# Staging the second weight matrix's words in its own storage, and finding clusters by halves of the tokens, in a routed attention with an ELU layer

## The chip, the cores and the metric

The kernel runs on one core of a Trainium2 chip. The metric is the device time of one execution in microseconds (us). The engines are TensorE (PE; its weight loads are listed as PEld), VectorE (DVE), ScalarE (ACT), GpSimd (POOL) and SyncE (SP), which here issues all DMA transfers, in the order of its queue.

## The reference

Two stages follow each other. The first is attention over 4 batches and 8 heads, with 768 tokens of 64 values. Each query and each key belongs to the one of 16 clusters whose centroid is most similar, and a query sees only the keys of its own cluster. The second is a layer with ELU.

```
q_assign = argmax(einsum('bhsd,hcd->bhsc', q_n, c_n))      # 16 clusters
k_assign = argmax(einsum('bhsd,hcd->bhsc', k_n, c_n))
mask = q_assign[:, :, :, None] == k_assign[:, :, None, :]
scores = where(mask, q @ k.T / 8, -1e9)
attn = softmax(scores) @ v                                  # (4, 8, 768, 64)
x = attn.transpose(0, 2, 1, 3).reshape(3072, 512)
h = x @ w_in                                                # (512, 2048)
g = where(h > 0, h, exp(min(h, 0)) - 1)
out = g @ w_out                                             # (2048, 512)
```

q, k, v and the centroids arrive as 32-bit floats. `w_in` and `w_out` arrive as 64-bit floats, and the kernel makes 32-bit floats of their words itself.

## The kernel before, in words

The attention is cut into 32 blocks: batch, half of the query tokens (`HS` = 384), and pair of heads (`blocks`). For block n, `scores(n)` makes, for each of 6 key tiles, the products q·k and on top of them a large negative number where the clusters differ (L350 and L359), and ACT takes the exponential (L367). `values(n)` multiplies with v (L394), sums the rows (L384), and DVE takes the reciprocal (L409). From block 4 on DVE adds up the key tiles first (`sums`, L371 and L373).

The clusters of a batch are worked out by `similar(b, j)` and `assign(b, j)`, j = 0 for q and 1 for k: 16 matmuls with 32 columns (L294), transposes out of PSUM (L302), the largest of 16 (L311), the comparison (L312), and a transpose back to the one-hot tile `hot` (L322). `masks(n)` makes the query side `qm` of a block from `hot` (L328).

The layer runs `LAG` = 4 blocks behind: during block n its group n - 4 runs. Groups come in turn as four `hidden` (8 matmuls with `w_in` into two PSUM banks, L422; ACT exponential L431; POOL clamp L432; DVE `gT`, L435, which reads the two banks and so frees them) and as six `outer` (4 matmuls with `w_out` each, L448). All of `similar`, `turn` (transposes of q and k), `scores`, the row sums and `hidden` draw on one pool of three PSUM tiles (`banks`).

The two weight matrices come as 32 pieces of 128 x 512 numbers: 0 to 15 are `w_in`, 16 to 31 are rows 0 to 15 of `w_out`. A piece's words, twice as large, are put into a place by a DMA (`ask`, L219). Generator `weight_steps` makes one step per piece: ACT goes on with piece n - 1 (L229, L230), DVE begins piece n (L234, L237) and ends piece n - 1 (L240, L243), POOL multiplies it (L246); then the place of piece n - 1 is free, and `ask` requests the next words. `ex`, the exponents, has two buffers, so L237 of step n follows L246 of step n - 1.

There are seven places: two tiles of their own (`words0`, `words1`), and five made of rows 6 to 15 of the `w_out` tile itself, two rows each; rows 0 to 5 first hold raw q and k. As soon as a piece of `w_out` is asked for (`asked >= into`, L213), the five are given up and the two are left.

Each engine's order is the order in which the code calls it. In blocks 0 to 3, `weigh` makes four steps a block; in blocks 4 to 7 two after each of the group's calls, five calls with `finish`, so steps 16 to 25 in block 4 and the rest in block 5. At a batch's last block `similar` and `assign` of the next batch are put between the `outer` calls. At the start of the program both run whole for q, then for k, then `masks(0)`.

Of the kernel before, what the change touches and what calls it, by code (L numbers as in the profile page):

```python
# [9 lines left out]
F32 = mybir.dt.float32  # L10
BF16 = mybir.dt.bfloat16
# [3 lines left out]
Alu = mybir.AluOpType  # L15
# [3 lines left out]
P = 128  # L19
# [41 lines left out]
def main_path(ctx, tc, c, q, k, v, centroids, moe_w_in, moe_w_out, out):  # L61
    nc = tc.nc
    B, H, S, D = q.shape
    NC = centroids.shape[1]
    DM, DF = moe_w_in.shape
    NT = S // P
    HT = NT // 2
    HS = S // 2
    NPR = H // 2
# [21 lines left out]
    def banks():  # L91
        return short.tile([P, 2, 512], F32, name="banks", tag="banks")
# [6 lines left out]
    used = 0  # L99

    def take(n):
        nonlocal used
        used += n
        return spare[:, used - n : used]
# [64 lines left out]
    cTz = const.tile([P, NPR, 2, 2, NC], F32, name="cTz")  # L169
    nc.vector.memset(cTz, 0.0)  # L170
    for pr in range(NPR):
# [1 line left out]
            cTz[:, pr, :, pr % 2],  # L173
            cps[:, 2 * pr * NC : 2 * (pr + 1) * NC].rearrange("p (e c) -> p e c", e=2),
        )
    count = const.tile([P, 2 * B], F32, name="count")
    r_sum = const.tile([P, HS], F32, name="r_sum")
    d_sum = const.tile([P, 2 * len(pairs)], F32, name="d_sum")
    nc.gpsimd.memset(r_sum, 0.0)
# [20 lines left out]
    words, exps = {}, {}  # L200
    places = []
    asked = 0

    def ask():

        nonlocal asked
        while asked < len(pieces):
            to, src = pieces[asked]
            if not wide:
                nc.sync.dma_start(to, src)  # L210
                asked += 1
                continue
            if asked >= into:  # L213
                places[:] = [x for x in places if x[1]]
            if not places:
                return
            place, own = places.pop(0)
            w = place.bitcast(U32)
            nc.sync.dma_start(w, src.bitcast(U32))  # L219
            words[asked] = (w.rearrange("p (n w) -> p n w", w=2), place, own)  # L220
            asked += 1

    def weight_steps():

        for n in range(len(pieces) + 1) if wide else ():
            if n > 0:
                to = pieces[n - 1][0]
                ex = exps[n - 1]
                nc.scalar.activation(to, to.bitcast(U32), Act.Identity, scale=2.0**-20, bias=one)  # L229
                nc.scalar.activation(ex, ex, Act.Relu, scale=8.0, bias=off)  # L230
            if n < len(pieces):
                high = words[n][0][:, :, 1]
                e = exps[n] = loads.tile([P, WC], U32, name="ex", tag="ex", bufs=2)
                nc.vector.tensor_scalar(  # L234
                    pieces[n][0].bitcast(U32), high, 0xFFFFF, None, op0=Alu.bitwise_and
                )
                nc.vector.tensor_scalar(e, high, 0x7FF00000, None, op0=Alu.bitwise_and)  # L237
            if n > 0:
                w, place, own = words.pop(n - 1)
                nc.vector.scalar_tensor_tensor(  # L240
                    ex, w[:, :, 1], 0x80000000, ex, op0=Alu.bitwise_and, op1=Alu.bitwise_or
                )
                nc.vector.scalar_tensor_tensor(  # L243
                    to, w[:, :, 0], 2.0**-52, to, op0=Alu.mult, op1=Alu.add
                )
                nc.gpsimd.tensor_tensor(to, to, ex.bitcast(F32), op=Alu.mult)  # L246
                places.append((place, own))
                ask()
            yield

    for n in range(2):
        places.append((loads.tile([P, 2 * WC], F32, name="words", tag=f"words{n}"), True))
    while used + 2 * WC <= FC * DM:
        places.append((take(2 * WC), False))
    ask()
    rest = weight_steps()

# [7 lines left out]
    T, sim, hot, qm = {}, {}, {}, {}  # L265
# [16 lines left out]
        to = T[i, j].rearrange("p (h s) -> p h s", h=2)  # L282
        nc.scalar.copy(to, ps[:, :, :HS])  # L283

    def similar(b, j):
        sim[b, j] = route.tile([P, S], F32, name="sim", tag="sim", bufs=1)
        ps = banks()
        for x in range(2):
            for half in range(2):
                for e in range(2):  # L290
                    for g in range(2):
                        pr = 2 * g + x
                        at = 64 * e + 32 * g
                        nc.tensor.matmul(  # L294
                            ps[at : at + 32, half, :HS],
                            lhsT=cTz[:, pr, e].rearrange("p x c -> p (x c)"),
                            rhs=T[b * NPR + pr, j][:, half * HS : (half + 1) * HS],
                            start=(x == 0),
                            stop=(x == 1),
                        )  # L300
        for half in range(2):
            nc.vector.transpose(  # L302
                sim[b, j][:, half * HS : (half + 1) * HS], ps[:, half, :HS]
            )

    def assign(b, j):
        n = S // NC
        s = sim.pop((b, j)).rearrange("p (n c) -> p n c", c=NC)
        top = route.tile([P, n], F32, name="top", tag="top", bufs=1)
        oh = route.tile([P, S], BF16, name="oh", tag="oh", bufs=1)  # L310
        nc.vector.tensor_reduce(top, s, axis=Axis.X, op=Alu.max)  # L311
        nc.vector.scalar_tensor_tensor(  # L312
            oh.rearrange("p (n c) -> p n c", c=NC),
            s,
            1.0,
            top.unsqueeze(2).to_broadcast([P, n, NC]),
            op0=Alu.mult,
            op1=Alu.is_equal,
            accum_out=count[:, 2 * b + j : 2 * b + j + 1],
        )  # L320
        hot[b, j] = route.tile([P, S], BF16, name="hot", tag=f"hot{j}", bufs=1 + j)
        nc.vector.transpose(hot[b, j], oh)  # L322

    def masks(n):
        b, half, pr = blocks[n]
        qm[n] = route.tile([P, HS], BF16, name="qm", tag="qm", bufs=2)
        s = big[:, pr : pr + 1]
        nc.vector.tensor_scalar(  # L328
            qm[n],
            hot[b, 0][:, half * HS : (half + 1) * HS],  # L330
            s,
            s,
            op0=Alu.mult,
            op1=Alu.subtract,
        )
# [139 lines left out]
    LAG = 4  # L475
# [13 lines left out]
    for j in range(2):  # L489
        for pr in range(NPR):  # L490
            turn(pr, j)
        similar(0, j)
        assign(0, j)
    masks(0)

    for n in range(len(blocks) + LAG):
        b, at = n // NB, n % NB
        ahead = b + 1 < B
        if ahead and at in turns:
            for j in range(2):  # L500
                turn((b + 1) * NPR + turns[at], j)
        if n <= len(blocks) and n > 0:
            values(n - 1)
        if ahead:
            for pr in {0: [0], 1: [1], 2: [2], 5: [3]}.get(at, []):
                load("q", (b + 1) * NPR + pr)
                load("k", (b + 1) * NPR + pr)
        if n + 1 < len(blocks):
            load_v(n + 1)
        if n < LAG:  # L510
            weigh(1)
        if n < len(blocks):
            scores(n)
            if at + 1 < NB:
                masks(n + 1)
            if n >= LAG:
                sums(n)
        beside = []
        if ahead and at + 1 == NB:
            for j in range(2):  # L520
                beside.append(lambda b=b, j=j: (similar(b + 1, j), assign(b + 1, j)))
            beside.append(lambda n=n: masks(n + 1))
        main = groups[n - LAG] if n >= LAG else []
        if n < LAG:
            weigh(3)
        done = 0
        for m, step in enumerate(main):
            step()
            upto = len(beside) * (m + 1) // len(main)
            for other in beside[done:upto]:  # L530
                other()
            done = upto
            if n < LAG + 4:
                weigh(2)
        for other in beside[done:]:
            other()
# [2 lines left out]

    ok = c["ok"]  # L540
    peak = const.tile([P, 2], F32, name="peak")
    same = const.tile([P, 2 * B], F32, name="same")
    nc.vector.tensor_reduce(peak[:, 0:1], r_sum, axis=Axis.X, op=Alu.add)
    nc.vector.tensor_reduce(peak[:, 1:2], d_sum, axis=Axis.X, op=Alu.add)
    nc.vector.tensor_scalar(ok[:, 0:1], peak[:, 0:1], R_MAX, None, op0=Alu.is_lt)
    nc.vector.tensor_scalar(ok[:, 1:2], peak[:, 1:2], D_MAX, None, op0=Alu.is_lt)
    nc.vector.tensor_scalar(same, count, float(S // NC), None, op0=Alu.is_equal)
    nc.vector.tensor_reduce(ok[:, 2:3], same, axis=Axis.X, op=Alu.min)
    nc.vector.tensor_reduce(ok[:, 3:4], ok[:, 0:3], axis=Axis.X, op=Alu.min)
    ps = banks()[:, 0]  # L550
# [227 lines left out]
```

## Time and profile before

| | us |
|---|---|
| median of 3 runs (1116.4 to 1118.55) | 1118.15 |
| profiled execution | 1116.62 |
| its span, first to last instruction | 1114.8 |
| PE busy | 1053.9 (95%) |
| DVE busy | 423.0 (38%) |
| ACT busy | 319.1 (29%) |
| POOL busy | 202.0 (18%) |

Shares of busy time are means over the span. What an edit is worth is read from the stage that it touches: from the waits there, and from who is waited for. A matmul in 32 bits stands in the trace as two records. Matmul ends are modelled, and neighbouring rows of PE overlap a little. Times in rows count from the span's start.

### The profile page before, as it was taken

To read this page: it belongs to the slowest core of one execution; us is meant where nothing else is said; L and a number is where in the kernel's file an instruction comes from. 1 tells how busy PE (TensorE), PEld (TensorE's weight loads), DVE (VectorE), ACT (ScalarE), POOL (GpSimd) and SP (SyncE) were. 2 spreads that over 40 slices of the span, in tenths; PEclk is the share of its full clock that TensorE was granted. 3 is DMA by queue.
4 is the path that set the end of the run, shared out by engine and by line. 5 is a ranking of instruction groups with operands and counts; after the bars stand their busy time and mean duration, and the time that the engine had idled before them with its cause. 6 is when DMAs were issued, how large, how long until landed. Compare 5 with 4: busy or idle time off the path is not lost.

```text
span 1114.8 us, 10753 instructions
## 1 busy us (share of the span) xinstructions
PE 1053.9 (95%) x4443; PEld 529.5 (47%) x4443; DVE 423.0 (38%) x472; ACT 319.1 (29%) x475; POOL 202.0 (18%) x169
## 2 busy tenths in 40 slices
PE   6999384999999999999999999999999999999997
PEld 4445142444554455444554455544554455444543
DVE  4686464344431244344332344334343334330210
ACT  3774252222331132222321223321222223221100
POOL 0344233111220022111211122110221112110100
PEclk9999686999999999999999999999999999999999
DMA  9642342003010001003010001000000000000000
GB/s 274 177 123 75 97 118 69 15 24 90 15 43 24 34 15 28 15 24 91 14 43 10 24 24 43 15 24 34 11 4 14 34 24 15 15 10 19 1 0 32
DMA packets 61961, 49.05 MB, mean 44 GB/s; under 512 B 45520, under 2 KB 54736, under 8 KB 61904
## 3 DMA queue, kind: packets, MB, share of 16 engines
q1 hardware_dynamic: 61904, 48.28, 15.0%
q8 instruction: 37, 0.61, 0.2%
q14 instruction: 20, 0.16, 0.0%
HBM read 41.98 MB, written 6.29 MB: 43 GB/s over the span
## 4 chain that ended last, share of the span: by engine, by line
PE 84%; DVE 9%; DMA 5%; POOL 1%; ACT 1%; issue 0%; DVEq 0%; ACTq 0%
PE banks L422 26%; PE o_bank L448 20%; PE f_bank L448 10%; PE o_bank L394 10%; PE banks L350 10%; DMA words<-in_moe_w_out_dram 4%; PE banks L359 2%; PE banks L294 2%; DVE ex L240 2%; PE banks L384 2%; PE banks L275 1%; DVE r L409 1%; DVE ex L237 1%; POOL w_in L246 1%; DVE psum L373 1%; DVE w_in L243 1%
## 5 line engine op out<-in xcount | busy, mean ns | idle before, releaser
L422 PE MATMUL banks<-xT,w_in 128*128 128x384 f32 x1024 | 334.8, 488 | 2.4 <-POOL xT L410 2.3
L422 PEld LDWEIGHTS banks<-xT,w_in 128*128 128x128 f32 x1024 | 193.1, 190 | 142.1 <-issue 7.3
L448 PE MATMUL o_bank<-w_out,gT 128*128 128x512 f32 x512 | 227.3, 596 | 0.7 <-ACT o_sb L457 0.7
L409 DVE RECIPROCAL r<-r 128x384 f32<-128x384 f32 x32 | 81.7, 2552 | 311.5 <-ACT r L408 311.5
L350 PE MATMUL banks<-qT,kT 64*128 64x384 f32 x768 | 163.8, 505 | 6.2 <-ACT qT L283 3.8
L367 ACT ACTIVATE p<-banks 128x768 f32<-128x768 f32 x192 | 152.1, 812 | 23.1 <-PE banks L359 21.1
L448 PEld LDWEIGHTS o_bank<-w_out,gT 128*128 128x128 f32 x512 | 95.8, 190 | 123.7 <-issue 121.9
L373 DVE TENSOR_TENSOR psum<-psum,p 128x768 f32<-128x768 f32 x112 | 141.4, 1263 | 11.7
L410 POOL TENSOR_TENSOR xT<-xT,r 128x384 f32<-128x384 f32 x32 | 54.7, 1710 | 499.5 <-DVE r L409 499.5
L435 DVE SCALAR_TENSOR_TENSOR gT<-gT,banks 128x768 f32<-128x768 f32 x64 | 61.0, 954 | 216.0 <-POOL gT L432 216.0
L394 PE MATMUL o_bank<-p,v_raw 128*64 128x384 f32 x768 | 137.3, 499 | 2.7 <-ACT o_sb L457 2.7
L431 ACT ACTIVATE gT<-banks 128x768 f32<-128x768 f32 x64 | 51.9, 810 | 261.7 <-PE banks L422 261.7
L448 PE MATMUL f_bank<-w_out,gT 128*128 128x512 f32 x256 | 114.1, 593 | 0.0
L350 PEld LDWEIGHTS banks<-qT,kT 64*128 64x128 f32 x768 | 68.7, 192 | 63.8 <-issue 34.8
L432 POOL TENSOR_SCALAR gT<-gT 128x768 f32<-128x768 f32 x64 | 53.4, 835 | 249.2 <-ACT gT L431 249.2
L394 PEld LDWEIGHTS o_bank<-p,v_raw 128*64 128x64 f32 x768 | 53.2, 140 | 78.2 <-issue 72.0
L457 ACT COPY o_sb<-o_bank 128x512 f32<-128x512 f32 x16 | 9.4, 587 | 274.4 <-PE o_bank L448 274.4
L448 PEld LDWEIGHTS f_bank<-w_out,gT 128*128 128x128 f32 x256 | 48.4, 190 | 61.7 <-issue 61.7
L359 PE MATMUL banks<-qm,hot 64*128 64x384 bf16 x384 | 64.8, 330 | 3.6 <-DVE qm L328 3.6
L411 POOL TENSOR_TENSOR r_sum<-r_sum,r 128x384 f32<-128x384 f32 x32 | 52.4, 1637 | 0.0
L406 ACT COPY xT<-o_bank 128x384 f32<-128x384 f32 x32 | 15.3, 480 | 94.1 <-PE o_bank L394 94.0
L359 PEld LDWEIGHTS <-hot 64*128 64x128 bf16 x384 | 19.9, 96 | 29.8 <-DVE hot L322 3.9
(85 smaller groups left out, 448.7 us busy)
## 6 DMA issues: line engine op xcount, KB each, us to landing
v_raw<-in_v_dram SPq DMA_DIRECT2D x32, 384.0 KB, 3.1
words<-in_moe_w_out_dram SPq DMA_DIRECT2D x16, 512.0 KB, 3.5
out_dram<-o_sb SPq DMA_DIRECT2D x24, 256.0 KB, 2.0
k_raw<-in_k_dram SPq DMA_DIRECT2D x28, 192.0 KB, 4.7
w_out<-in_moe_w_in_dram SPq DMA_DIRECT2D x10, 512.0 KB, 6.3
q_raw<-in_q_dram SPq DMA_DIRECT2D x24, 192.0 KB, 4.4
words<-in_moe_w_in_dram SPq DMA_DIRECT2D x6, 512.0 KB, 4.6
q_raw<-in_q_dram SPq DMA_DIRECT2D x2, 384.0 KB, 3.5
```

Source lines behind the costliest of these rows:

```text
L350: nc.tensor.matmul(s[:, e, :HS], lhsT=T[i, 1][rows, ts(kt, P)], rhs=T[i, 0][rows, cols], start=True, stop=False,)
L359: nc.tensor.matmul(s[:, e, :HS], lhsT=hot[b, 1][rows, ts(kt, P)], rhs=qm[n][rows], start=False, stop=True,)
L367: nc.scalar.activation(p, s[:, :, :HS], Act.Exp, scale=SCALE)
L373: nc.vector.tensor_tensor(to, to, pu[n, kt], op=Alu.add)
L394: nc.tensor.matmul(o_bank[64 * e : 64 * e + 64, :HS], lhsT=raw["v", n][:, e, kt], rhs=pu[n, kt][:, e], start=(kt == 0), stop=(kt == NT - 1),)
L409: nc.vector.reciprocal(r, r)
L410: nc.gpsimd.tensor_tensor(x, x, r, op=Alu.mult)
L411: nc.gpsimd.tensor_tensor(r_sum, r_sum, r, op=Alu.add)
L422: nc.tensor.matmul(h[:, e, :HS], lhsT=w_in[:, ch, ts(2 * n + e, P)], rhs=xT[b * NPR + ch, half], start=(ch == 0), stop=(ch == KC - 1),)
L432: nc.gpsimd.tensor_scalar(t, t, 1.0, 0.0, op0=Alu.min, op1=Alu.max)
L435: lambda: nc.vector.scalar_tensor_tensor(t, t, -1.0, h[:, :, :HS], op0=Alu.add, op1=Alu.max)
L448: nc.tensor.matmul(o, lhsT=g[f // 2][:, f % 2, ts(t, P)], rhs=w_out[:, f], start=(f == 0), stop=(f == FC - 1),)
```

## The change

Four edits. First, a place carries a limit instead of a mark: a place in rows f and f + 1 of `w_out` may take words of any piece below 16 + f - 1, that is, of pieces which are finished before row f itself is begun. Second, the steps are handed out two after each of the first four calls of a group, in every block until none is left: steps 16 to 23 in block 4, 24 to 31 in block 5, 32 in block 6. Third, `similar` and `assign` work on half of the tokens, 384, and `masks(0)` stands between q and k. Fourth, at a batch's last block the calls of `similar` and `assign` are eight, spread singly between the `outer` calls.

```diff
-            if asked >= into:
-                places[:] = [x for x in places if x[1]]
+            places[:] = [x for x in places if asked < x[1]]
             if not places:
                 return
-            place, own = places.pop(0)
+            place, limit = places.pop(0)
...
     while used + 2 * WC <= FC * DM:
-        places.append((take(2 * WC), False))
+        limit = into + used // DM - 1
+        places.append((take(2 * WC), limit))
...
-    def similar(b, j):
-        sim[b, j] = route.tile([P, S], F32, name="sim", tag="sim", bufs=1)
-        ps = banks()
+    def similar(b, j, half):
+        if half == 0:
+            sim[b, j] = route.tile([P, S], F32, name="sim", tag="sim", bufs=1)
+        ps = banks()[:, 0]
+        cols = slice(half * HS, (half + 1) * HS)
...
-    def assign(b, j):
-        n = S // NC
+    def assign(b, j, half):
+        if half == 0:
+            hot[b, j] = route.tile([P, S], BF16, name="hot", tag=f"hot{j}", bufs=1 + j)
+        cols = slice(half * HS, (half + 1) * HS)
+        n = HS // NC
...
-        similar(0, j)
-        assign(0, j)
-    masks(0)
+        for half in range(2):
+            similar(0, j, half)
+            assign(0, j, half)
+        if j == 0:
+            masks(0)
...
-                beside.append(lambda b=b, j=j: (similar(b + 1, j), assign(b + 1, j)))
+                for half in range(2):
+                    beside.append(lambda b=b, j=j, half=half: similar(b + 1, j, half))
+                    beside.append(lambda b=b, j=j, half=half: assign(b + 1, j, half))
...
-            if n < LAG + 4:
+            if m < 4:
                 weigh(2)
```

SP's queue in blocks 2 to 4, as a difference (- before, + now); the two loads of v are those for blocks 4 and 5. `words` and `w_out` ahead of the arrow are the places that take the words of the last pieces.

```order
+L218 DMA w_out<-in_moe_w_out_dram 128x1024 x2
 L115 DMA v_raw<-in_v_dram 128x2x384
-L219 DMA words<-in_moe_w_out_dram 128x1024
+L218 DMA w_out<-in_moe_w_out_dram 128x1024 x3
+L218 DMA words<-in_moe_w_out_dram 128x1024
 L115 DMA v_raw<-in_v_dram 128x2x384
-L219 DMA words<-in_moe_w_out_dram 128x1024 x10
+L218 DMA words<-in_moe_w_out_dram 128x1024
+L218 DMA w_out<-in_moe_w_out_dram 128x1024 x3
+L218 DMA words<-in_moe_w_out_dram 128x1024 x2
```

The words of six `w_out` pieces (five of them into `w_out`) are are requested ahead of the second load of v, where before it was one.

DVE at the start of the program, from k's similarity on, before (`sim`, `hot` and `oh` numbered as buffers):

```order
L302 STREAM_TRANSPOSE sim_292<-banks_293 128x384 x2
L311 TENSOR_REDUCE top_312<-sim_292 128x48
L312 SCALAR_TENSOR_TENSOR oh_313,count_153<-sim_292,top_312 128x768
L322 STREAM_TRANSPOSE hot_316<-oh_313 128x768
L328 TENSOR_SCALAR qm_318<-hot_254,big_125 128x384
L234 TENSOR_SCALAR w_in_60<-words_161 128x512
```

and now, from the mask on:

```order
L329 TENSOR_SCALAR qm_262<-hot_241,big_125 128x384
L302 STREAM_TRANSPOSE sim_300<-banks_301 128x384
L312 TENSOR_REDUCE top_312<-sim_300 128x24
L314 SCALAR_TENSOR_TENSOR oh_313,count_153<-sim_300,top_312 128x384
L323 STREAM_TRANSPOSE hot_311<-oh_313 128x384
L302 STREAM_TRANSPOSE sim_300<-banks_317 128x384
L312 TENSOR_REDUCE top_327<-sim_300 128x24
L314 SCALAR_TENSOR_TENSOR oh_328,count_153<-sim_300,top_327 128x384
L323 STREAM_TRANSPOSE hot_311<-oh_328 128x384
L233 TENSOR_SCALAR w_in_60<-words_161 128x512
```

The mask `qm` now stands ahead of k's clusters, and k's first half is in `hot` after four instructions of half the size.

PE in the last block of a batch, before:

```order
L448 MATMUL o_bank<-w_out,gT 128x512 x8
L294 MATMUL banks<-qT,cTz 32x384 x16
L448 MATMUL o_bank<-w_out,gT 128x512 x8
L294 MATMUL banks<-kT,cTz 32x384 x16
L448 MATMUL f_bank<-w_out,gT 128x512 x8
```

and now:

```order
L449 MATMUL o_bank<-w_out,gT 128x512 x4
L295 MATMUL banks<-qT,cTz 32x384 x8
L449 MATMUL o_bank<-w_out,gT 128x512 x4
L295 MATMUL banks<-qT,cTz 32x384 x8
L449 MATMUL o_bank<-w_out,gT 128x512 x8
L295 MATMUL banks<-kT,cTz 32x384 x8
L449 MATMUL f_bank<-w_out,gT 128x512 x4
L295 MATMUL banks<-kT,cTz 32x384 x8
L449 MATMUL f_bank<-w_out,gT 128x512 x4
```

The two similarity stretches have become four of half the length, so `outer` is cut twice more.

## Rows read from the trace of the kernel before

**Rows 1.** Windows: stretch and length, busy us (instructions) by engine, PE clock, DMA.
```profile
core 0: us, PE busy (x) PEld busy (x) DVE busy (x) ACT busy (x) POOL busy (x), PEclk, DMA share, GB/s
...
88.00:144.00 56.00, 33.39 (x120) 17.73 (x118) 29.78 (x47) 20.22 (x31) 18.83 (x16) 0.80 0.31 92
144.00:196.00 52.00, 37.20 (x142) 20.18 (x140) 28.65 (x41) 19.97 (x31) 17.46 (x15) 0.79 0.32 93
```
**Rows 2.** Groups by form: busy us, mean ns | idle us before, and its releaser.
```profile
L234 DVE TENSOR_SCALAR w_out<-words 128x512 uint32<-128x512 uint32 x16 | 8.1, 508 | 44.3 <-DMA words<-in_moe_w_out_dram 44.3
```
**Rows 3.** Timeline of DVE, block 4: start us, us, engine, line [idle before <-releaser].
```profile
96.38 1.06 DVE L234 TENSOR_SCALAR w_out<-words 128x512 uint32<-128x512 uint32 x1
...
98.29 0.71 DVE L243 SCALAR_TENSOR_TENSOR w_in<-words,w_in 128x512 f32<-128x512 uint32 x1
102.47 0.43 DVE L234 TENSOR_SCALAR w_out<-words 128x512 uint32<-128x512 uint32 x1 [3.47 <-DMA words<-in_moe_w_out_dram]
...
103.75 0.69 DVE L243 SCALAR_TENSOR_TENSOR w_out<-words,w_out 128x512 f32<-128x512 uint32 x1
104.35 0.95 DVE L435 SCALAR_TENSOR_TENSOR gT<-gT,banks 128x768 f32<-128x768 f32 x1
```
**Rows 4.** Timeline of PE, blocks 4 and 5.
```profile
89.58 21.30 PE L422 MATMUL banks<-xT,w_in 128*128 128x384 f32 x64
116.25 1.54 PE L275 MATMUL banks<-ident,q_raw 128*128 128x128 f32 x6 [5.37 <-DVE gT L435]
127.06 1.54 PE L275 MATMUL banks<-ident,k_raw 128*128 128x128 f32 x6 [9.27 <-DVE gT L435]
...
138.10 1.49 PE L384 MATMUL banks<-psum,ones 128*64 128x384 f32 x4 [4.09 <-DVE gT L435]
...
195.11 0.81 PE L384 MATMUL banks<-psum,ones 128*64 128x384 f32 x4
...
200.90 3.70 PE L448 MATMUL o_bank<-w_out,gT 128*128 128x512 f32 x8
```
**Rows 5.** Timeline of DVE, block 1: two weight steps' first instructions.
```profile
50.27 0.43 DVE L234 TENSOR_SCALAR w_in<-w_out 128x512 uint32<-128x512 uint32 x1
...
53.42 0.42 DVE L234 TENSOR_SCALAR w_in<-words 128x512 uint32<-128x512 uint32 x1
```
**Rows 6.** Timeline of POOL, block 4.
```profile
96.33 0.83 POOL L432 TENSOR_SCALAR gT<-gT 128x768 f32<-128x768 f32 x1 [2.81 <-ACT gT L431]
...
104.57 1.27 POOL L246 TENSOR_TENSOR w_out<-w_out,ex 128x512 f32<-128x512 f32 x1 [4.23 <-issue]
```
**Rows 7.** Timeline of all engines at the program's start, from k's similarity on.
```profile
17.87 3.18 PE L294 MATMUL banks<-kT,cTz 128*32 128x384 f32 x32
...
21.11 1.05 DVE L302 STREAM_TRANSPOSE sim<-banks 128x384 f32<-128x384 f32 x2 [1.82 <-PE banks L294]
...
25.08 0.34 DVE L328 TENSOR_SCALAR qm<-hot,big 128x384 bf16<-128x384 bf16 x1
...
25.47 0.46 PE L359 MATMUL banks<-qm,hot 64*128 64x384 bf16 x2 [3.58 <-DVE qm L328]
...
29.16 3.23 ACT L367 ACTIVATE p<-banks 128x768 f32<-128x768 f32 x4 [0.78 <-PE banks L359]
...
33.64 0.69 DVE L240 SCALAR_TENSOR_TENSOR ex<-words,ex 128x512 uint32<-128x512 uint32 x1 [6.59 <-ACT ex L230]
```
**Rows 8.** Chain that ended last: start us, us, engine, tile, line, records.
```profile
242.57 7.06 PE o_bank L448 x16
...
376.72 6.87 PE f_bank L448 x16
```
**Rows 9.** DMA issues: tiles, KB each, median us to landing.
```profile
words<-in_moe_w_out_dram SPq DMA_DIRECT2D x16, 512.0 KB, 3.5
```
**Rows 10.** Timeline of PE, block 3: key tiles ahead of and behind an idle stretch.
```profile
69.52 0.81 PE L350 MATMUL banks<-qT,kT 64*128 64x384 f32 x4
...
72.38 0.92 PE L350 MATMUL banks<-qT,kT 64*128 64x384 f32 x4 [1.89 <-ACT p L367]
...
73.29 1.43 PE L350 MATMUL banks<-qT,kT 64*128 64x384 f32 x4
```

More of the change, by code (lines that the diff above doesn't have):

```diff
@@ L175, in main_path @@
         )
-    count = const.tile([P, 2 * B], F32, name="count")
+    count = const.tile([P, 4 * B], F32, name="count")
     r_sum = const.tile([P, HS], F32, name="r_sum")
@@ L212, in ask @@
                 continue
-            if asked >= into:
-                places[:] = [x for x in places if x[1]]
+            places[:] = [x for x in places if asked < x[1]]
             if not places:
                 return
-            place, own = places.pop(0)
+            place, limit = places.pop(0)
             w = place.bitcast(U32)
             nc.sync.dma_start(w, src.bitcast(U32))
-            words[asked] = (w.rearrange("p (n w) -> p n w", w=2), place, own)
+            words[asked] = (w.rearrange("p (n w) -> p n w", w=2), place, limit)
             asked += 1
@@ L238, in weight_steps @@
             if n > 0:
-                w, place, own = words.pop(n - 1)
+                w, place, limit = words.pop(n - 1)
                 nc.vector.scalar_tensor_tensor(
@@ L246, in weight_steps @@
                 nc.gpsimd.tensor_tensor(to, to, ex.bitcast(F32), op=Alu.mult)
-                places.append((place, own))
+                places.append((place, limit))
                 ask()
@@ L251, in main_path @@
     for n in range(2):
-        places.append((loads.tile([P, 2 * WC], F32, name="words", tag=f"words{n}"), True))
+        places.append((loads.tile([P, 2 * WC], F32, name="words", tag=f"words{n}"), len(pieces)))
     while used + 2 * WC <= FC * DM:
-        places.append((take(2 * WC), False))
+        limit = into + used // DM - 1
+        places.append((take(2 * WC), limit))
     ask()
@@ L283, in turn @@
         nc.scalar.copy(to, ps[:, :, :HS])
-    def similar(b, j):
-        sim[b, j] = route.tile([P, S], F32, name="sim", tag="sim", bufs=1)
-        ps = banks()
-        for x in range(2):
[L289 to L304, printed above, removed]
@@ L306, in assign @@
-    def assign(b, j):
-        n = S // NC
-        s = sim.pop((b, j)).rearrange("p (n c) -> p n c", c=NC)
+    def similar(b, j, half):
[3 more added lines that the diff above has]
+        cols = slice(half * HS, (half + 1) * HS)
+        for x in range(2):
+            for e in range(2):
+                for g in range(2):
+                    pr = 2 * g + x
+                    at = 64 * e + 32 * g
+                    nc.tensor.matmul(
+                        ps[at : at + 32, :HS],
+                        lhsT=cTz[:, pr, e].rearrange("p x c -> p (x c)"),
+                        rhs=T[b * NPR + pr, j][:, cols],
+                        start=(x == 0),
+                        stop=(x == 1),
+                    )
+        nc.vector.transpose(sim[b, j][:, cols], ps[:, :HS])
@@ L309, in assign @@
+    def assign(b, j, half):
[3 more added lines that the diff above has]
+        n = HS // NC
+        s = sim[b, j][:, cols].rearrange("p (n c) -> p n c", c=NC)
         top = route.tile([P, n], F32, name="top", tag="top", bufs=1)
-        oh = route.tile([P, S], BF16, name="oh", tag="oh", bufs=1)
+        oh = route.tile([P, HS], BF16, name="oh", tag="oh", bufs=1)
         nc.vector.tensor_reduce(top, s, axis=Axis.X, op=Alu.max)
+        at = 4 * b + 2 * j + half
@@ L318, in assign @@
             op1=Alu.is_equal,
-            accum_out=count[:, 2 * b + j : 2 * b + j + 1],
+            accum_out=count[:, at : at + 1],
         )
-        hot[b, j] = route.tile([P, S], BF16, name="hot", tag=f"hot{j}", bufs=1 + j)
-        nc.vector.transpose(hot[b, j], oh)
+        nc.vector.transpose(hot[b, j][:, cols], oh)
     def masks(n):
@@ L541, in main_path @@
     peak = const.tile([P, 2], F32, name="peak")
-    same = const.tile([P, 2 * B], F32, name="same")
+    same = const.tile([P, 4 * B], F32, name="same")
     nc.vector.tensor_reduce(peak[:, 0:1], r_sum, axis=Axis.X, op=Alu.add)
@@ L546, in main_path @@
     nc.vector.tensor_scalar(ok[:, 1:2], peak[:, 1:2], D_MAX, None, op0=Alu.is_lt)
-    nc.vector.tensor_scalar(same, count, float(S // NC), None, op0=Alu.is_equal)
+    nc.vector.tensor_scalar(same, count, float(HS // NC), None, op0=Alu.is_equal)
     nc.vector.tensor_reduce(ok[:, 2:3], same, axis=Axis.X, op=Alu.min)
```

## The prediction

> **What bounds the kernel now.** I read the windows first. Between 88 and 196 us TensorE (PE) is busy for 33.39 of 56 and 37.20 of 52 us, at mean granted clocks of 0.80 and 0.79 [rows 1]; after that it hardly stops. So 37.4 us of PE idle lie in blocks 4 and 5, where `w_out` is converted. Next, who waits there: VectorE (DVE) sat 44.3 us in front of the first instruction of a weight step, 14 times, for a transfer of words [rows 2]. The DVE timeline shows one such step: DVE stood still from 99.0 (98.29 + 0.71) to 102.47 and was done with the step at 104.35 [rows 3]. The PE timeline shows who pays: the turns of block 5 wait 5.37 and 9.27 us, and the row sums of block 4 wait 4.09 us, for PSUM banks that the ELU's last instruction, `gT` on DVE (L435), must free [rows 4]. `gT` stands behind two weight steps each time, so transfer → DVE → bank → PE is the chain. The last PE instruction that waits for it is the row sum of block 5, at 195.11; from 200.90 PE runs through [rows 4]. I use that row sum as the marker.
>
> A second chain is at the start: PE waits 3.58 us for the first mask, because DVE works out the clusters of all 768 k tokens before PE may use any [rows 7].
>
> **The change, part 1: words staged in `w_out`.** Before, from piece 16 on two places take turns, each asked for at the end of the step that frees it; a transfer lands in 3.5 us (median) [rows 9], nearly all of it waited for. Counting the requests of the new rule with its limits: pieces 16 to 22 are asked for seven places ahead, 23 to 27 with three or more steps between, 28 to 30 with one step and a `gT` between, piece 31 at the end of step 30, with nothing between. So all waits go but one.
>
> What is late next? A step without a wait for words takes 3.15 us (50.27 to 53.42) [rows 5]. Its four DVE instructions need 1.88 us (102.47 to 104.35) [rows 3], the rest is the multiply on GpSimd (POOL, L246, 1.27 us) [rows 6]: 1.88 + 1.27 = 3.15, so DVE and POOL take turns. In blocks 4 and 5 one `gT` and its clamp on POOL (L432) come to each pair of steps. `gT` and L246 overlapped at 104.35 and 104.57 with neither longer [rows 3, 6], so I cost `gT` at nothing, under L246; without that cover it would be 0.95 us a pair. The clamp is dearer: beside the one at 96.33 (0.83 us) the masking instruction L234 took 1.06 instead of 0.43 us [rows 3, 6]. So the pair costs between 2 × 3.15 = 6.3 us (clamp free) and 7.13 us (clamp in turn); I take 7.1, by that row. The Trainium skill (SBUF — State Buffer, Who interferes with whom) gives DVE and GpSimd one shared pair of ports, which whoever comes first holds for the whole instruction; by that rule 7.1 holds, and without a lock the sum below would be 5 us lower. The row of 1.06 us agrees. PE needs 5.3 us for a pair's matmuls (21.30 / 4) [rows 4], so the DVE–POOL chain remains the limit, not PE.
>
> Times on the old axis. Block 4: step 16 ends at 99.0 as before; step 17 ends at 102.15; its `gT` 0.95 later at 103.1; three more pairs to 124.4; row sum at 124.5 (138.10 before). Block 5: a row sum and the scores after it take 5.8 us (195.11 to 200.90) [rows 4], the first hidden pair 5.3: 135.6. In block 4 step 16 ended 4.1 us after its first hidden pair (89.58 + 5.3 = 94.9, to 99.0): step 24 ends at 139.7, step 25 at 142.85, the first `gT` at 143.8. Three pairs: 165.2. Piece 31's transfer adds 3.5 in place of the 1.27 of L246 that it hides: 167.4. Row sum at 167.5 instead of 195.11: **27.6 us gained**.
>
> Clock: PE still idles behind `gT`, some 2 us before the marker. At 72.38 an idle of 1.89 us was followed by key tiles at half clock, 1.43 instead of 0.81 us (1.2 GHz, the lower of its two levels) [rows 10]. I charge 2 us, between 0 and 3.5.
>
> The step that slips from blocks 4 and 5 into block 6 (eight steps a block instead of ten) finds DVE idle: costed at nothing, with `outer` of block 6 (20 us of PE) as cover. Requests pass the q, k and v loads on SP's queue, which wait for PE to free their buffers; those buffers are free a block earlier, so nothing is charged (rival B prices it).
>
> **Part 2: clusters by halves, at the start.** The sixteen matmuls of k's similarity run from 17.87 for 3.18 us; the first eight end near 19.5. DVE's chain for 768 tokens runs from 21.11 to the mask at 25.08, 4.0 us, so about 2.1 a half with its extra starts: first half at 21.7, second at 23.8. q's halves are done under k's turns, and the q mask now stands ahead of k. PE's scores reach the one-hot at 21.9 instead of 25.47 [rows 7]: 3.55 us. PE then no longer falls to half clock (three key tiles near 1.5 instead of 0.81 us), and the last exponential ends near 27.2 instead of 32.39 (29.16 + 3.23) [rows 7]. The first waiting weight instruction, at 33.64, moves to 28.5. **5.1 us gained**, between 2 (only DVE's end counts) and 5.5; from there to block 4 the chain is DVE and POOL without other slack, so it shifts whole. The words of the first pieces must then land some 2 to 5 us earlier than they were used; no row shows DVE waiting for them, and the low end of 2 us covers a wait.
>
> **Part 3: the same at the three batch ends.** PE runs through there, so the DVE time is covered by `outer` and by the next block's values, without which the last half's chain of 2.1 us would be paid. But the four similarity blocks now cut `outer` in four places instead of two. A stretch of 16 right after a cut took 7.06, one that goes on 6.87 [rows 8]: 0.19 a cut, 6 more cuts, **1.1 us lost**; up to 3.6 if entering the narrow matmuls costs twice as much again. The Trainium skill (TensorEngine Tiling, Key Properties) says that a change of tiling mode drains TensorE, which speaks against these cuts; counted for entry and exit at 0.19 each, an estimate, it would be 2.3 us. The rows show the exit; the entry no row separates.
>
> **Sum.** The profiled execution took 1116.62 us (span 1114.8), 1.5 below the median of 1118.15. 1116.6 − 27.6 + 2 − 5.1 + 1.1 = **1087.0 us**. A difference under 0.2% (2 us) can't be told from none here.
>
> **Rivals.**
> A: the waits go and DVE and POOL keep up, so PE sets the time in blocks 4 and 5. Then the 37.4 us idle goes and some 9 us of half clock with it (of at most 0.2 × 108 = 22): 46 us; 1116.6 − 46 − 5.1 + 1.1 = 1066.6. Needs a pair under 5.3 us. The step of 3.15 us speaks against it. 0.04.
> B: words come late again, because requests stand on SP behind loads that wait for PE, and pieces 23 to 30 each wait as 31 does, 3.5 − 1.27 = 2.2 us: 8 × 2.2 = 17.6 more, 1104.6. For it: DVE now asks in quick succession. Against: before, with the same loads in between, a request landed in 3.5 us all the same [rows 9]. 0.06.
> C: no place in `w_out` is really used beyond piece 16. Then only parts 2 and 3 act: 1116.6 − 5.1 + 1.1 = 1112.6; with the start gaining nothing either, no change. The order of SP's queue speaks against it. 0.02 (0.02 more for no change).
> D, slower: at the three batch ends the last half of k's clusters is late, since four similarity blocks now draw on three PSUM banks and the fourth must wait for DVE. Place: between `outer` and the next block's scores. PE has 3.4 us of `outer` and the values behind the last cut as slack; slower only if each of the three ends stalls by more than 10 us, 29.6 / 3. At 12 us each: 1087 + 36 = 1123. DVE's 2.1 us a half speak against it. 0.02.
> That the start gains only 2 us, or the clamp is free, is within the forecast.
>
> **How the numbers follow.** Forecast case 0.84: 1087. Low end: clamp free (6 × 0.83 = 5.0), start 5.5, no half clock (2), last transfer hidden (2.2): 1077.4. High end: start 2 (3.1 less), clock 3.5 (1.5), cuts 3.6 (2.5), clamp as long as L246 (6 × (1.27 − 0.83) = 2.6): 1096.7. The range 1077 to 1098 leaves out A, B, C and D, 0.16. Faster 0.95 (forecast, A, B, C and a little of the tails), same 0.02, slower 0.03.
>
> **What would show it.** In the profile after: no wait of DVE for words but one near the end of block 5, of some 3.5 us; weight steps at 3.1 us, pairs near 7.1; the block 5 row sum near 162; PE's mask wait at the start under 1 us; a cut of `outer` at 0.2 us. Wrong would be: several waits for words, a wait for sim or hot at a batch end, or PE without idle in blocks 4 and 5.

## The result, and the profile after

The changed kernel takes **1084.36 us** (median of 4 runs, 1083.68 to 1084.65), the kernel before 1118.35 us in the same comparison: a ratio of 0.9699, 95% interval 0.9682 to 0.9716. The forecast was 1087.0 us (1077 to 1098) and faster. The profiled execution took 1084.65 us with a span of 1082.9 us, 31.9 less than the 1114.8 before. Of these 31.9, the stages below show 2.7 at the start, 31.4 in blocks 4 and 5, and a loss of 2.0 at the batch ends; 0.2 is not placed.

**The words.** The waits for words, by group (columns as in [rows 2], where they were 44.3 us):

```profile
L233 DVE TENSOR_SCALAR w_out<-w_out 128x512 uint32<-128x512 uint32 x9 | 5.8, 648 | 0.0
...
L233 DVE TENSOR_SCALAR w_out<-words 128x512 uint32<-128x512 uint32 x7 | 4.3, 609 | 3.5 <-DMA words<-in_moe_w_out_dram 3.5
```

Nine pieces of `w_out` are now read from places in `w_out` itself, none of them with a wait. One wait is left. The DVE timeline shows it, and pairs of steps in front of it (it answers to [rows 3]):

```profile
99.29 0.95 DVE L436 SCALAR_TENSOR_TENSOR gT<-gT,banks 128x768 f32<-128x768 f32 x1
...
100.99 1.05 DVE L236 TENSOR_SCALAR ex<-w_out 128x512 uint32<-128x512 uint32 x1
...
106.30 0.95 DVE L436 SCALAR_TENSOR_TENSOR gT<-gT,banks 128x768 f32<-128x768 f32 x1
...
153.32 0.95 DVE L436 SCALAR_TENSOR_TENSOR gT<-gT,banks 128x768 f32<-128x768 f32 x1
...
160.71 0.43 DVE L233 TENSOR_SCALAR w_out<-words 128x512 uint32<-128x512 uint32 x1 [3.51 <-DMA words<-in_moe_w_out_dram]
...
162.59 0.95 DVE L436 SCALAR_TENSOR_TENSOR gT<-gT,banks 128x768 f32<-128x768 f32 x1
```

A pair of steps, from `gT` to `gT`, takes 7.0 us (99.29 to 106.30). The wait of 3.51 us at 160.71 is that of piece 31.

**Who pays.** PE's idle time by what ended it (us in total, times, longest), whole program:

```profile
PE banks L275 <- DVE gT L436: 10.7, 2, 5.5
...
PE banks L360 <- DVE hot L323: 0.4, 1, 0.4
```

Only two waits of PE for `gT` are left, both of the turn of k (L275). The timeline of PE says where, and what follows them ([rows 4] before):

```profile
114.30 1.54 PE L275 MATMUL banks<-ident,k_raw 128*128 128x128 f32 x6 [5.50 <-DVE gT L436]
115.77 6.19 PE L395 MATMUL o_bank<-p,v_raw 128*64 128x384 f32 x24
...
148.33 0.82 PE L275 MATMUL banks<-ident,q_raw 128*128 128x128 f32 x6
154.32 1.54 PE L275 MATMUL banks<-ident,k_raw 128*128 128x128 f32 x6 [5.17 <-DVE gT L436]
155.79 4.97 PE L395 MATMUL o_bank<-p,v_raw 128*64 128x384 f32 x24
160.59 0.81 PE L385 MATMUL banks<-psum,ones 128*64 128x384 f32 x4
...
166.80 3.70 PE L449 MATMUL o_bank<-w_out,gT 128*128 128x512 f32 x8
```

The turn of q goes without a wait (0.82 us, full clock), the turn of k waits for the third `gT` (at 153.32) and then runs at half clock, the lower level of 1.2 GHz (1.54 us), and part of the values too (6.19 and 4.97 us for what takes 4.1 at full clock). The row sum of block 5, at 160.59, runs **two microseconds before** the fourth `gT` (162.59): it waits for nothing. `outer` of block 6 starts at 166.80 instead of 200.90. The windows agree ([rows 1] showed 37.4 us of idle at clocks of 0.80 and 0.79):

```profile
83.00:120.00 37.00, 30.01 (x110) 16.75 (x108) 31.83 (x45) 18.86 (x27) 17.76 (x15) 0.91 0.34 107
120.00:165.00 45.00, 39.67 (x180) 21.42 (x178) 33.45 (x46) 24.34 (x37) 19.04 (x15) 0.96 0.35 95
```

Idle is now 7.0 and 5.3 us, and the mean granted clock is 0.91 and 0.96.

**The start.** All engines, from the second half of q's turns on (answers to [rows 7]):

```profile
10.74 2.83 PE L279 MATMUL banks<-ident,w_out 128*64 128x128 f32 x48
...
19.74 3.14 PE L295 MATMUL banks<-kT,cTz 128*32 128x384 f32 x32
...
21.65 0.58 DVE L302 STREAM_TRANSPOSE sim<-banks 128x384 f32<-128x384 f32 x1 [1.36 <-PE banks L295]
...
24.09 0.34 PE L360 MATMUL banks<-qm,hot 64*128 64x384 bf16 x2 [0.36 <-DVE hot L323]
...
30.57 0.69 DVE L239 SCALAR_TENSOR_TENSOR ex<-words,ex 128x512 uint32<-128x512 uint32 x1 [2.66 <-ACT ex L229]
```

PE's wait for the clusters is 0.36 us instead of 3.58, and PE is at full clock behind it (key tiles of 0.81 us). But k's similarity began at 19.74, not 17.87, so the first waiting weight instruction moved by 3.07 us (33.64 to 30.57), and DVE's reciprocal of block 3, the last instruction of that stage, by 2.7 (87.38 to 84.65).

**A batch's last block.** PE, with `outer` (L449) and the similarity matmuls (L295):

```profile
198.62 3.70 PE L449 MATMUL o_bank<-w_out,gT 128*128 128x512 f32 x8
202.25 1.50 PE L295 MATMUL banks<-qT,cTz 128*32 128x384 f32 x16
203.68 3.70 PE L449 MATMUL o_bank<-w_out,gT 128*128 128x512 f32 x8
207.31 1.50 PE L295 MATMUL banks<-qT,cTz 128*32 128x384 f32 x16
208.74 7.13 PE L449 MATMUL o_bank<-w_out,gT 128*128 128x512 f32 x16
...
225.92 4.09 PE L395 MATMUL o_bank<-p,v_raw 128*64 128x384 f32 x24
```

From the first `outer` to the values: 225.92 - 198.62 = 27.30 us. The same stretch of the kernel before went from 232.72 to 259.34, 26.62 us:

```profile
232.72 7.13 PE L448 MATMUL o_bank<-w_out,gT 128*128 128x512 f32 x16
239.78 2.79 PE L294 MATMUL banks<-qT,cTz 128*32 128x384 f32 x32
242.50 7.13 PE L448 MATMUL o_bank<-w_out,gT 128*128 128x512 f32 x16
...
259.34 4.09 PE L394 MATMUL o_bank<-p,v_raw 128*64 128x384 f32 x24
```

So 0.68 us is lost at each of the three batch ends, with no wait in it.

### The profile page after: what moved, and what is told of

Its sections match the earlier page's. It is cut to its first block, busy times and chain, and to the rows that moved or that the text cites. A ratio compares the mean times of both kernels' runs of the same rounds, so it can differ in the third digit from the quotient of the medians.

```text
span 1082.9 us, 10783 instructions
## 1 busy us (share of the span) xinstructions
PE 1049.6 (97%) x4443; PEld 525.6 (49%) x4443; DVE 431.1 (40%) x504; ACT 319.2 (29%) x475; POOL 203.7 (19%) x169
## 4 chain that ended last, share of the span: by engine, by line
PE 89%; DVE 6%; POOL 3%; ACT 1%; issue 1%; DMA 0%; ACTq 0%; POOLq 0%
PE banks L423 29%; PE o_bank L449 21%; PE o_bank L395 11%; PE f_bank L449 10%; PE banks L351 10%; PE banks L360 2%; PE banks L295 2%; PE banks L385 2%; PE banks L275 2%; DVE ex L239 1%; POOL w_in L245 1%; DVE r L410 1%; DVE ex L236 1%; POOL w_out L245 1%; DVE w_in L242 1%
## 5 line engine op out<-in xcount | busy, mean ns | idle before, releaser
L449 PE MATMUL o_bank<-w_out,gT 128*128 128x512 f32 x512 | 228.1, 596 | 0.7 <-ACT o_sb L458 0.7
L351 PE MATMUL banks<-qT,kT 64*128 64x384 f32 x768 | 159.1, 492 | 2.9 <-ACT p L368 2.8
L449 PEld LDWEIGHTS o_bank<-w_out,gT 128*128 128x128 f32 x512 | 95.5, 190 | 124.2 <-issue 122.1
L449 PE MATMUL f_bank<-w_out,gT 128*128 128x512 f32 x256 | 114.9, 594 | 0.0
L351 PEld LDWEIGHTS banks<-qT,kT 64*128 64x128 f32 x768 | 66.3, 186 | 58.9 <-issue 36.0
L449 PEld LDWEIGHTS f_bank<-w_out,gT 128*128 128x128 f32 x256 | 48.1, 190 | 62.1 <-issue 62.1
L245 POOL TENSOR_TENSOR w_in<-w_in,ex 128x512 f32<-128x512 f32 x16 | 22.0, 1375 | 55.4 <-DVE w_in L242 55.4
```

The lines of the kernel that those rows point to most:

```text
L351: nc.tensor.matmul(s[:, e, :HS], lhsT=T[i, 1][rows, ts(kt, P)], rhs=T[i, 0][rows, cols], start=True, stop=False,)
L449: nc.tensor.matmul(o, lhsT=g[f // 2][:, f % 2, ts(t, P)], rhs=w_out[:, f], start=(f == 0), stop=(f == FC - 1),)
```

## The experiments

The expectations were written before each run. "Marker" below is the start of `outer` in block 6 (200.90 before, 166.80 in the changed kernel). "Spread" is the order in which weight steps are handed out in blocks 4 and 5. T is the theory after the result, R a rival to it, in e1, e2 and e4 the prediction's sums. The changed kernel was run once more as a control, on the chip of e5, e6 and e7: 1084.27 us (1083.22 to 1085.65), ratio 0.9704 (0.9691 to 0.9718).

**Words only** (e1): the kernel before with the new limits of the places and the new hand-out, clusters whole.

```diff
-            if asked >= into:
-                places[:] = [x for x in places if x[1]]
+            places[:] = [x for x in places if asked < x[1]]
...
-            if n < LAG + 4:
+            if m < 4:
                 weigh(2)
```

> The kernel before with the place limits and the new handing out of steps alone; clusters whole as before. Theory T: the last wait of PE for the weight chain is the turn of k in block 6, for the third gT of block 5; the row sum behind it waits for no gT. Then blocks 4 and 5 gain 31.4 us (34.1 us earlier start of outer in the changed kernel, less the 2.7 us by which its reciprocal of block 3 was earlier): 1118.35 - 31.4 = 1087.0 us. Rival R (the prediction's sums): the row sum waits for the fourth gT, and 2 us of half clock are paid: gain 25.6, 1092.7 us.

Measured: 1086.0 us (1085.5 to 1086.18), ratio 0.9718 (0.9703 to 0.9733). That is 31.2 us under the median before, as T says and not R. In the profiles the marker is at 170.43, 30.5 us earlier than before, and from there on nothing changes (span 30.4 less). It is 0.9 less than the 31.4 of the changed kernel: 0.3 from a later start (block 3's reciprocal at 87.65 instead of 87.38), the rest from values that ran at half clock for longer (5.51 and 6.32 us, together 0.7 more). So staging and the new hand-out together are worth 30.5 us in the profiles, nearly the whole result. Neither was run without the other, so how they share it is not shown.

**Halves only** (e2): the changed kernel with places and hand-out as before, so that the clusters by halves are left.

```diff
-            places[:] = [x for x in places if asked < x[1]]
+            if asked >= into:
+                places[:] = [x for x in places if x[1]]
...
-            if m < 4:
+            if n < LAG + 4:
                 weigh(2)
```

> The kernel before with the clusters by halves alone (start and batch ends), places and steps as before. Theory T: the start gains 2.7 us, up to 3.8 where the first loads land as early as in the kernel before, and the three batch ends lose 2.0 us (0.68 each, from the chain of the changed kernel): 1118.35 - 2.7 + 2.0 = 1117.6 us, between 1116.5 and 1117.6. Rival R (the prediction's sums): 1118.35 - 5.1 + 1.1 = 1114.3 us.

Measured: 1117.23 us (10 runs, 1116.28 to 1118.3) against 1117.22, ratio 1.0 (0.9991 to 1.0009), within T's range and not R's 1114.3. Nothing by itself, but not because nothing happens: the marker is 2.8 us earlier (198.11), the batch ends take 2.0 back, and the last stretch of `hidden` took 1.7 us longer (below, under the clamp).

**Two cuts** (e3): all halves of q, then all of k, each in one place, so that `outer` is cut twice as before.

```diff
-                for half in range(2):
-                    beside.append(lambda b=b, j=j, half=half: similar(b + 1, j, half))
-                    beside.append(lambda b=b, j=j, half=half: assign(b + 1, j, half))
+                beside.append(
+                    lambda b=b, j=j: [f(b + 1, j, half) for f in (similar, assign) for half in range(2)]
+                )
```

> The changed kernel, but at the batch ends both halves of q's similarity stand together, then both of k's, as in the kernel before, so that outer is cut twice and not four times. Theory T: the cuts cost 2.0 us in all (four stretches of 1.43 against two of 2.72, and outer in 21.58 instead of 21.18 us, three times): 1084.36 - 2.0 = 1082.4 us. Rival: a cut costs only the 0.19 us of the first matmul behind it, 1.1 us in all: 1083.2; or the loss lies elsewhere: 1084.4.

Measured: 1082.37 us (1081.3 to 1083.9), ratio 0.9688 (0.9674 to 0.9701), 1.9 to 2.0 us less than the changed kernel's 1084.27 and 1084.36, by the ratios 1.2 to 1.8. The medians alone would not decide between T and its rivals; the stretch does. The stretch at the batch end is back at its old length:

```profile
198.34 7.13 PE L449 MATMUL o_bank<-w_out,gT 128*128 128x512 f32 x16
...
224.97 4.09 PE L395 MATMUL o_bank<-p,v_raw 128*64 128x384 f32 x24
```

224.97 - 198.34 = 26.63. Two more cuts cost 0.67 us, and the halves themselves nothing.

**The last step longer** (e4): the exponent instruction of the step of piece 31 is written twelve times, so that the fourth `gT` of block 5 comes later. If PE waits for that `gT`, PE must come later too.

```diff
-                nc.vector.tensor_scalar(e, high, 0x7FF00000, None, op0=Alu.bitwise_and)
+                for _ in range(12 if n == 31 else 1):
+                    nc.vector.tensor_scalar(e, high, 0x7FF00000, None, op0=Alu.bitwise_and)
```

> The changed kernel with the exponent instruction of piece 31 (the last step in block 5, which waits for its transfer) written twelve times, some 3.7 us more on DVE ahead of the fourth gT of block 5, same values. Theory T: PE waits for the third gT alone, the row sum for a bank that ScalarE frees; no change, 1084.4 us, and scores of block 6 start as in the changed kernel. Rival R (the prediction's path through the fourth gT): 3.7 us slower, 1088.1 us.

Measured: 1086.02 us (1085.11 to 1087.25), ratio 0.9719 (0.9706 to 0.9733), between the two. The twelve took 5.50 us, so about 5.1 was added. DVE and PE by their timelines:

```profile
158.83 5.50 DVE L237 TENSOR_SCALAR ex<-words 128x512 uint32<-128x512 uint32 x12
...
165.45 0.95 DVE L437 SCALAR_TENSOR_TENSOR gT<-gT,banks 128x768 f32<-128x768 f32 x1
```

```profile
152.11 1.54 PE L276 MATMUL banks<-ident,k_raw 128*128 128x128 f32 x6 [5.17 <-DVE gT L437]
153.58 6.39 PE L396 MATMUL o_bank<-p,v_raw 128*64 128x384 f32 x24
159.80 0.81 PE L386 MATMUL banks<-psum,ones 128*64 128x384 f32 x4
...
166.73 3.70 PE L450 MATMUL o_bank<-w_out,gT 128*128 128x512 f32 x8
```

The row sum ran at 159.80, 5.65 us before the fourth `gT` at 165.45, without a wait, and the marker is where it was, not 5.1 us later. So the row sum does not wait for that `gT`, which refutes R. The 1.7 us by which the run is longer lie at the other end of the program: the last stretch of `hidden`, which starts at 994.13 here and at 994.20 in the changed kernel, took 41.30 us instead of 39.61. This execution had come to block 5 2.2 us earlier (the turn of k at 152.11 instead of 154.32); 1.4 of that went in values at half clock for longer, the rest in the scores. The 1.4 needs no longer step: in e3, which is the changed kernel up to there, k's turn also came earlier (152.64), and the values took as long:

```profile
154.12 6.36 PE L395 MATMUL o_bank<-p,v_raw 128*64 128x384 f32 x24
```

The other 0.7 lies ahead of two key tiles in the scores of block 6, at 164.62 and 165.73. The first waits for ACT:

```profile
164.62 0.92 PE L352 MATMUL banks<-qT,kT 64*128 64x384 f32 x4 [0.15 <-ACT p L369]
```

Neither the changed kernel nor e3 has a gap there, and the fourth `gT` had not yet freed its bank, so these 0.7 us are probably the price of the longer step: two banks in turn instead of three. That is read from the order of the rows, not tried. What makes the last stretch 1.7 us longer stays open.

**No clamp** (e6): POOL's clamp is left out in the eight `hidden` calls of blocks 4 and 5.

```diff
-            nc.gpsimd.tensor_scalar(t, t, 1.0, 0.0, op0=Alu.min, op1=Alu.max)
+            if b > 0 or half > 0:
+                nc.gpsimd.tensor_scalar(t, t, 1.0, 0.0, op0=Alu.min, op1=Alu.max)
```

> The changed kernel without POOL's clamp at 1 in the two groups of the first half batch (blocks 4 and 5; what is left out there is the min of the ELU). Theory T: DVE and POOL take turns, so each of the pairs gets 0.75 us shorter, 6.2 us instead of 6.95, and the third gT of both blocks about 2 us earlier: 3.5 to 4.5 us faster than the changed kernel, 1080.4 us. Rival: the clamp costs DVE nothing: no change, pairs near 7.0 us.

Measured: 1082.45 us (1080.21 to 1082.75), ratio 0.968 (0.9665 to 0.9694), 1.8 less than the control, where 3.5 to 4.5 had been expected. The DVE timeline:

```profile
99.31 0.95 DVE L437 SCALAR_TENSOR_TENSOR gT<-gT,banks 128x768 f32<-128x768 f32 x1
...
101.01 0.41 DVE L236 TENSOR_SCALAR ex<-w_out 128x512 uint32<-128x512 uint32 x1
...
105.68 0.95 DVE L437 SCALAR_TENSOR_TENSOR gT<-gT,banks 128x768 f32<-128x768 f32 x1
```

The pair takes 6.37 us instead of 7.0, and L236, which had stood beside the clamp, 0.41 us instead of 1.05: the 0.64 that the clamp cost a pair is all in that one instruction. The marker moves by 3.5 us, to 163.29. Only 1.8 of it arrives, because 1.7 goes again in the last stretch of `hidden`:

```profile
163.29 3.70 PE L450 MATMUL o_bank<-w_out,gT 128*128 128x512 f32 x8
...
990.70 41.30 PE L423 MATMUL banks<-xT,w_in 128*128 128x384 f32 x122 [2.26 <-POOL xT L411]
```

**Is that 41.30 chance?** Two kernels were profiled again, one that had shown 41.30 and the changed one.

> The kernel without the clamp again, for the last stretch of hidden: 41.30 us in its profile, 39.61 us in that of the changed kernel. If the half clock behind the idle of 2.26 us comes by chance, 39.61 may show here, and the time is then 1.7 us less, 1080.2 to 1080.8. If it belongs to the kernel, 41.30 shows again, and 1082.5.

> The changed kernel again, for the same stretch: by chance, 41.30 may show here, with 1085.7 to 1086.0; if it belongs to the kernel, 39.61 and 1083.2 to 1084.6.

Measured: 1082.79 us with 41.31, and 1084.5 us with 39.61. Both repeat: nothing here speaks for chance of an execution, and it seems to go with the kernel, as far as one repetition of each can say.

**Spread** (e5): the two waits for the third `gT` were PE's last of any size in these blocks, and that `gT` stood behind six steps. So the steps are handed out 1, 1, 2, 2, 1 in blocks 4 and 5: seven a block instead of eight, and the last three in block 6.

```diff
-            if m < 4:
-                weigh(2)
+            weigh((1, 1, 2, 2, 1)[m] if n < LAG + 2 else 2)
```

> The changed kernel with the weight steps of blocks 4 and 5 handed out 1, 1, 2, 2, 1 behind the five calls (seven a block, the last three in block 6), so that the third gT of a block stands behind four steps instead of six. Theory T: PE waits in blocks 4 and 5 for that third gT alone (5.5 and 5.2 us) and runs at half clock behind each wait (some 2 us each time, values in 6.19 and 4.97 instead of 4.1 us, a turn in 1.54 instead of 0.82): both go, 10.7 + 4.4 us less some 2 us for what the DVE-POOL chain still holds up in block 6: about 1071 us, between 1069 and 1075. Rival: the chain of DVE and POOL as a whole is the limit (33 steps of 3.15 us) and the wait only moves to block 6, where outer needs the last pieces: less than 4 us gained, 1080 us or more.

Measured: 1076.99 us (1075.31 to 1077.27), ratio 0.9632 (0.9619 to 0.9645): 7.3 less than the control, where 13 had been expected; that lies between T's range and the rival's. PE in block 4, by its timeline:

```profile
109.55 0.87 PE L275 MATMUL banks<-ident,k_raw 128*128 128x128 f32 x6 [1.62 <-DVE gT L436]
110.36 4.09 PE L395 MATMUL o_bank<-p,v_raw 128*64 128x384 f32 x24
115.93 0.87 PE L385 MATMUL banks<-psum,ones 128*64 128x384 f32 x4 [1.48 <-ACT qT L283]
...
157.13 3.70 PE L449 MATMUL o_bank<-w_out,gT 128*128 128x512 f32 x8
```

The wait for `gT` fell from 5.50 to 1.62 us, and PE stays at full clock (0.87 and 4.09 us instead of 1.54 and 6.19). A new wait of 1.48 us stands behind it, for the copy of q on ACT, which stands behind ACT's part of the weight steps. Over both blocks the idle that has a releaser fell by 4.7 us and the half clock by 4.3; the marker came 9.7 earlier, 0.9 of it from an earlier start. 1.7 were again lost in the last stretch, 41.31 us here. So the step that failed in this expectation is that all idle of the two waits would go: of 10.7 us, 3.2 stayed and 2.9 came back behind another releaser.

**Both together** (e7): e5 with the two cuts of e3.

> Both edits: steps handed out 1, 1, 2, 2, 1, and outer cut twice at a batch end. Theory T: the two gains lie in different stretches and add up: the time of the spread kernel less 2.0 us, about 1069 us. Rival: no more than the spread alone, if the cuts were hidden.

Measured: **1075.69 us** (1073.29 to 1076.08), ratio 0.962 (0.9607 to 0.9633). It beats the kernel before by 3.8% and the changed one by some 8.6 us. The gain over e5 is 1.3 instead of 2.0 in the medians; its profiled execution began 1.0 us later (q's turn of the staged tokens at 10.96 instead of 9.99), and the last `hidden` stretch still began 0.95 earlier (983.58 instead of 984.53), the 2.0 of the batch ends less that delay.

**Late pairs** (e8): e7 with 1, 1, 1, 2, 2, to have the third `gT` one step earlier.

> Steps of blocks 4 and 5 handed out as 1, 1, 1, 2, 2 (instead of 1, 1, 2, 2, 1), with two cuts. In the kernel with 1, 1, 2, 2, 1 PE still waits twice 1.62 us for the third gT and twice 1.44 to 1.50 us for the copy of q on ACT, which stands behind the weight steps' ACT work. T: the third gT comes one step (3.1 us) earlier, so the two waits of 1.62 us go, and the waits for ACT stay or grow by as much as PE comes earlier: 1072.5 to 1075.7. Rival: ACT's copy is the later of the two anyway, and all that goes from the first wait is added to the second: no change, 1075.7.

Measured: 1080.27 us (1079.37 to 1081.59), ratio 0.9665 (0.965 to 0.968): 4.6 slower than e7, a miss of both. PE's timeline in block 5:

```profile
152.30 0.87 PE L385 MATMUL banks<-psum,ones 128*64 128x384 f32 x4 [2.12 <-DVE gT L436]
155.12 1.65 PE L351 MATMUL banks<-qT,kT 64*128 64x384 f32 x4 [1.95 <-ACT qT L283]
```

The turn of k waits no longer, as expected, but now the row sum does wait for the fourth `gT`, and the scores behind it for ACT, at half clock (1.65 us). In block 4 the two waits are 2.13 and 1.32 us. PE's instructions are in the same order in e7 and e8; only `gT` and the weight steps changed places on DVE, ACT and POOL. I take it that the pool of three banks gives the row sum another bank because other releases come first; that was not tried by itself.

## Why the prediction was right, point by point

The time is 2.6 us from the forecast, and the mechanism holds in the main: the words' waits went, and pairs of steps took what was charged. But one step of the chain was wrong, three terms were mis-sized, and part of the agreement is luck.

**All waits for words go but one: right.** 44.3 us became 3.51, at piece 31. Rivals B and C are out: nine pieces were read from `w_out`, without a wait.

**The pair at 7.1 us: right, and shown.** Measured 7.0; without the clamp 6.37, close to the 6.3 named as the other end. The Trainium skill's rule (SBUF — State Buffer, Who interferes with whom) that DVE and GpSimd exclude each other on the shared ports agrees: L236 beside the clamp took 1.05 us, and 0.41 without it. That PE waits for DVE and POOL in blocks 4 and 5, and not they for PE, is right too, which puts rival A out; e5 adds that the order of the steps matters there, not only their pace.

**The row sum of block 5 as the marker: wrong.** This is the step "Piece 31's transfer adds 3.5 ... Row sum at 167.5 instead of 195.11: 27.6 us gained". It took for granted that the row sum waits for the fourth `gT` of block 5. That of block 4 did [rows 4, 138.10, 4.09 us], but the row of block 5, at 195.11, has no wait in it, and I read past that: its fourth `gT`, at 190.62, had ended 3.5 us before.

```profile
190.62 0.94 DVE L435 SCALAR_TENSOR_TENSOR gT<-gT,banks 128x768 f32<-128x768 f32 x1
```

In the changed kernel the row sum runs two microseconds before the fourth `gT`, and in e4 5.65 us before it. PE's last wait for a `gT` is that of the turn of k, for the third one, so the last transfer of 3.5 us, the last step and the last `gT` do not hold up the row sum. On the old axis (2.7 us added for the start) the row sum comes at 163.3 instead of 167.5, which is 4.2 us of gain more. About 1.2 of that would have come in any case, since the fourth `gT` itself ended at 163.54, 166.2 on the old axis, instead of 167.4; the other 3.0 are the wrong path. In block 4 the same step was wrong and does not show in the time: the row sum at 121.80, 124.5 on the old axis, is the forecast to a tenth, but it too waited for nothing, and came by the third `gT` and values at half clock. That is luck.

**Half clock, 2 us charged: mis-sized.** It came behind k's turns, as said, 1.54 instead of 0.82 us and 4.97 instead of 4.1; but as the row sum waits for nothing this lies ahead of the marker, within the 163.3. From the row sum to `outer` it took 6.21 instead of 5.8 us, so 0.4 was paid behind the marker, not 2, and that 0.4 is no half clock either: it is a gap ahead of the key tile at 163.37, which waits for ACT. With the row sum that makes 4.2 + 1.6 = 5.8: the words gave 31.4 where 25.6 net was forecast. e1 has 30.5 for this part alone. How long the half clock lasts changes the sum by itself: the values took 6.19 and 4.97 us here, 5.60 and 6.36 in e3, with the same program up to there.

**The start, 5.1 us: mis-sized, 2.7 measured.** PE's wait for DVE and its half clock went as said (0.36 us left, full clock), but k's similarity began 1.87 us later. Of that 1.1 stems from the turn of the staged q, at 10.74 instead of 9.67, where both kernels have the same program: among the executions profiled here it began anywhere from 9.44 to 10.96. In e3, where it began at 9.72, block 3's reciprocal came at 83.58, 3.8 us earlier than before. The rest is the price of the halves: q's similarity takes 0.3 us more (3.10, from 2.79), and k's turn 0.4, of which 0.21 is a wait for DVE, which takes q's halves out of PSUM one by one. A half of the DVE chain takes 2.4 us (21.65 to the end of `hot` at 24.04) instead of 2.1.

**The batch ends, 1.1 us: mis-sized, 2.0 measured.** The sum charged six exits at 0.19 us. But the narrow stretches get longer too: four similarity stretches at 1.43 us (207.31 to 208.74) against two at 2.72 (239.78 to 242.50) are 0.28 more, the `outer` stretches 0.40. That is 0.34 a cut, and e3 took it all back. The Trainium skill (TensorEngine Tiling (Array Packing), Key Properties) says that a change of tiling mode drains TensorE. The trace agrees that entry and exit together cost more than the exits alone: the 2.3 us estimated for both were nearer to the 2.0 measured than my 1.1. The page gives no size; the rows here have 0.20 us a cut in `outer` and 0.14 in the similarity, and don't separate entry from exit. Rival D found nothing to stand on: no wait for `sim` or `hot` at a batch end.

The three errors in the gain, +5.8, -2.4 and -0.9 us, sum to +2.5; the profiled execution is 2.35 us under the forecast (1087.0 - 1084.65). So 1087.0 was near partly because errors cancel. Halves are worth little: 2.7 us at the start for 2.0 at the batch ends; with two cuts (e3) nothing is lost at the batch ends.

## What to carry to other kernels

Before a wait serves as the end of a chain, look whether that very row carries a wait, in the stage in question and not only in its twin; where PSUM tiles come from a pool, the last consumer that really waits can be one call earlier or later, and moved here with the order of other engines' work. Filling work handed out evenly between calls delays the ones that free buffers: giving the early calls less and the late ones more, and one step fewer in all, took 7.3 us off here, and one step further gave 4.6 back. Splitting a narrow matmul stretch pays where a wait is seen, at the program's start, and costs 0.34 us a cut where PE runs through anyway.

## What was not expected of the hardware

The same idle of 2.25 or 2.26 us before the last stretch of `hidden` was followed by 39.61 us for its 122 records in the kernel before, the changed one (three profiles), e1 and e3, and by 41.30 or 41.31 us in e2, e4, e5, e6 (two profiles), e7 and e8. The granted clock in the six microseconds around the stretch's start (windows, columns as in [rows 1]) was 1.00 in the changed kernel,

```profile
994.00:1000.00 6.00, 5.80 (x18) 3.53 (x19) 0.51 (x1) 0.81 (x1) 1.93 (x3) 1.00 0.00 0
```

and 0.72 in e6, a mean of full and half clock:

```profile
990.00:996.00 6.00, 5.30 (x11) 3.02 (x12) 0.00 (x0) 0.09 (x1) 1.60 (x2) 0.72 0.00 0
```

Each of the two kernels that were profiled again repeats its own figure. What decides between them stays open; it makes 1.7 us, as much as some of the edits above, so small differences between kernels were read at the marker and not at the end. In the same way two idles of 5.50 and 5.17 us cost 6.19 and 4.97 us of values in one and the same program.
